# Narrower one-hot blocks and larger bursts in a fused Fourier-mixing and expert kernel

## The chip, the cores and the metric

The kernel runs on one core of a Trainium2 chip. The metric is the device time of one execution in microseconds (us). Engines are named as in the profile: PE (TensorE, matrix multiply; PEld are its weight loads), DVE (VectorE), ACT (ScalarE), POOL (GpSimd) and SP (SyncE, which mostly issues DMAs). Lines L1 to L1303 are those of the kernel before, unless the text says that they are of the changed one.

## What is computed

The output is a gated sum of two branches on the same input x of 2048 tokens and 640 features.

```python
g = sigmoid((x * gate_w).sum(-1, keepdims=True))
a = dft_seq_re @ (x @ dft_hid_re.T) - dft_seq_im @ (x @ dft_hid_im.T)
# branch b, for each token and each of 32 heads:
s1 = q1 @ k1.T ; s2 = q2 @ k2.T        # 16 scores each
t1, i1 = top2(s1) ; t2, i2 = top2(s2)  # 4 pairs, expert i1 * 16 + i2 of 256
top_s, top_e = top2(t1[:, None] + t2)  # the best 2 of the 4 pairs
w = softmax(top_s)
b = sum over heads and 2 picks of w * gelu(x . u[top_e]) * v[top_e]
out = g * a + (1 - g) * b
```

The change lies in branch b, in one step. For every token, the 64 weights w (32 heads, 2 picks) have to be added up into a table of 16 x 16 experts, at row i1 and column i2 of each pick. Everything behind it (gelu, the product with v) then works on that dense table.

## The kernel before, in words

**Large matmuls.** Nearly all of PE's time goes into float32 products written as three matmuls on split operands (`mm3`, L143 to L145): a high times a high part, a high times a low, a low times a high. The order of the program is the order of the *pieces*: 128 pieces of the sequence transform, each with five groups of three matmuls of 512 columns (`seq_piece`), which accumulate in the PSUM banks 0 to 4. Sixteen pieces make one tile; at its end ACT copies the five banks into `ST` (L246), DVE multiplies them by the gate (L217), and ACT issues their stores (L227). Behind the pieces comes the hidden-dimension transform (`step`), which ends the kernel.

**Operands of a piece.** `load_piece` loads `wf` five pieces ahead (SP, L177). `split_piece` makes the high and the low part in `WS` three pieces ahead: either ACT and POOL (L138, L139), or ACT twice (L188, L189) and then a DMA issued by POOL which adds `wf` from DRAM (L191).

**Background work.** What is not a large matmul is written as generators and queued in a `Pump`. `run_bg(0.68)` after each group of three matmuls adds credit, and the pump takes the next step of a generator as long as there is credit; each step yields its price in us (the *charge*). So the charges decide between which matmuls a step's instructions are written into the program, and each engine then runs its own instructions in that order. `at(n, ...)` ties a step to piece n.

**The one-hot step** (`experts`, L802 to L886). `ROWS[g]` holds, for half g of the tokens, three numbers for each of 128 partitions (pick, head, and a split of the weight in two) and token: a power of two that stands for the row expert, one for the column expert, and the weight. A *set* is 64 tokens. `build` makes two f16 matrices of 1024 columns for a set with three DVE instructions (L845): each token's 16 columns say which power of two its number equals, and the row expert's matrix is also multiplied by the weight. `use` multiplies block by block on PE (L857): a block is four tokens, 16 x 4 = 64 columns, so a set is 16 matmuls of 64 columns with 64 output partitions, alternating between partitions 0 to 63 and 64 to 127. A block's product holds all 4 x 4 pairs of its tokens; only a token with itself is wanted. So ACT multiplies the bank by a mask, one column of tokens at a time (L815, four instructions of 128 elements for a set), and DVE adds over the four token columns (L821, one reduction for a set) into `cd`. `store_gates` (L796, SP) writes `cd` to DRAM.

Sets are used in bursts: three built sets give one burst of 48 matmuls on PE, in banks 6, 7 and 5, each set in a bank of its own. There are four set buffers in two tiles, `hot0` and `hot1`; the latter lies under the tag `WP`, which is needed from piece NPC - 4 on, so that groups have two sets near the end (`ending`). `settle`, called after every build instruction, writes the sum of one masked set and the mask of the next. `closing` holds masks back in the last piece of a tile, `early` tells of pieces below `ACCUM_END`, where builds are charged less.

Of the kernel before, what the change touches and what calls it, by code (L numbers as in the profile page):

```python
# [17 lines left out]
P = 128  # L18
# [23 lines left out]
AWAY = 11  # L42
BYPASS = 4
# [63 lines left out]
def gated_mix_kernel(ctx: ExitStack, tc: tile.TileContext, xT, xn, dreT, dimT, wsre, wsim, wq, kT, uT, vv, gw, out):  # L107
# [97 lines left out]
    p3, last_part, ending, closing, early, share = None, False, False, False, True, 0.95  # L205
# [133 lines left out]
    wtab4 = const.tile([P, E, 4], F16)  # L339
    powers = const.tile([P, E], F16)  # L340
    top_bits = const.tile([P, 1], F32)
    mask4 = const.tile([P, 4], F32)
# [9 lines left out]
    def make_tables():  # L352
        for e in range(E):
            nc.gpsimd.memset(powers[:, e:e + 1], 2.0 ** (E - 1 - e))
        nc.gpsimd.memset(top_bits, INF)
        nc.gpsimd.tensor_copy(wtab4, powers[:, :, None].to_broadcast([P, E, 4]))
        nc.vector.tensor_reduce(mask4, identf.rearrange("p (a b) -> p b a", b=4), op=OP.add, axis=AX.X)
        nc.vector.tensor_scalar(mask4, mask4, 1.0 / GSCALE, None, op0=OP.mult)
# [443 lines left out]
    def experts():  # L802


        shp = [P, 16, E, 4]
        wt = wtab4[:, None].to_broadcast(shp)
# [5 lines left out]
        def mask(t):  # L812
            f = t.rearrange("p m (e t) -> p (m e) t", t=4)
            for n in range(4):
                nc.scalar.activation(f[:, :, n], f[:, :, n], AF.Copy, scale=mask4[:, n:n + 1])  # L815

        def add_up(g, c, t):
# [3 lines left out]
            nc.vector.tensor_reduce(cd[g][:, :, 8 * c:8 * c + 8].rearrange("p e m -> p m e"),  # L821
                                    t.rearrange("p m (e t) -> p m e t", e=E), op=OP.add, axis=AX.X)
            if c == 15:
# [11 lines left out]

        def build(g, c, s):
            pt, qt = (HOT[s // 2][:, s % 2, n].rearrange("p (m e t) -> p m e t", e=E, t=4) for n in range(2))

            def row(n):
                r = ROWS[g][:, n, 8 * c:8 * c + 8, :].rearrange("p b (s t) -> p (b s) t", t=4)  # L840
# [3 lines left out]
            for o, a, b, op in ((pt, row(0), wt, OP.is_equal), (qt, row(1), wt, OP.is_equal), (pt, pt, row(2), OP.mult)):  # L844
                nc.vector.tensor_tensor(o, a, b, op=op)  # L845
                yield (0.8 if early else 1.05) + settle()

        def use(group):
# [3 lines left out]
            for i, (g, c, s) in enumerate(group):  # L852
                t = bank((6, 7, 5)[i], (P, 8, E * 4))
                pt, qt = (HOT[s // 2][:, s % 2, n].rearrange("p (m c) -> p m c", m=16) for n in range(2))
                for m in range(16):
                    r = slice(64 * (m % 2), 64 * (m % 2) + 64)
                    nc.tensor.matmul(t[r, m // 2, :], pt[:, m], qt[:, m], start=True, stop=True)  # L857
# [446 lines left out]
```

## Time and profile before

| | |
|---|---|
| median of 3 executions | 750.1 us (749.87 to 751.22) |
| the profiled execution | 750.43 us |
| span of its instructions | 748.7 us |
| granted PE clock | 0.999 |
| PE / PEld busy | 743.8 / 603.8 us |
| DVE / ACT / POOL busy | 585.7 / 365.9 / 342.4 us |
| matmuls of the one-hot step (L857) | 512, from 419.6 to 587.6 us |
| builds, masks, sums (L845, L815, L821) | 96, 128, 32 instructions |

The span runs from the first to the last instruction on the engines; 1.7 us lie around it. Busy time counts instructions on an engine, also those that overlap in its pipeline, so that a busy PE is not PE at its peak. In a row of a group stand the line, the engine and operation, what is written and read, the count, then busy us and mean ns of one, then the engine's idle time ahead of them and what ended it. In a row of the chain or of the timeline stand start and length in us.

### The profile page before, as it was taken

To read this page: it belongs to the slowest core of one execution; us is meant where nothing else is said; L and a number is where in the kernel's file an instruction comes from. 1 tells how busy PE (TensorE), PEld (TensorE's weight loads), DVE (VectorE), ACT (ScalarE), POOL (GpSimd) and SP (SyncE) were. 2 spreads that over 40 slices of the span, in tenths; PEclk is the share of its full clock that TensorE was granted. 3 is DMA by queue.
4 is the path that set the end of the run, shared out by engine and by line. 5 is a ranking of instruction groups with operands and counts; after the bars stand their busy time and mean duration, and the time that the engine had idled before them with its cause. 6 is when DMAs were issued, how large, how long until landed. Compare 5 with 4: busy or idle time off the path is not lost.

```text
span 748.7 us, 11141 instructions
## 1 busy us (share of the span) xinstructions
PE 743.8 (99%) x3925; PEld 603.8 (81%) x3925; DVE 585.7 (78%) x741; ACT 365.9 (49%) x664; POOL 342.4 (46%) x286
## 2 busy tenths in 40 slices
PE   9999999999999999999999999999999999999998
PEld 7777767888888888888888888888888888888887
DVE  6964098495999899999999888979899974357651
ACT  4325234543544745555463686633545653443451
POOL 5533325440532424145235456643455793487253
PEclk9999999999999999999999999999999999999999
DMA  9999999777556786972398766488876689775301
GB/s 333 392 380 364 344 374 354 231 222 250 129 176 141 190 242 157 237 200 79 114 395 285 162 168 188 133 255 280 266 234 197 222 262 343 219 239 172 113 29 71
DMA packets 84488, 171.11 MB, mean 229 GB/s; under 512 B 16080, under 2 KB 21328, under 8 KB 84176
## 3 DMA queue, kind: packets, MB, share of 16 engines
q1 hardware_dynamic: 70960, 146.13, 57.9%
q0 software_dynamic: 5472, 9.96, 8.5%
q10 hardware_dynamic: 8000, 14.31, 5.2%
q8 instruction: 31, 0.51, 0.3%
q14 instruction: 25, 0.20, 0.1%
HBM read 136.40 MB, written 32.39 MB: 225 GB/s over the span
## 4 chain that ended last, share of the span: by engine, by line
PE 94%; DMA 5%; SPq 0%; DVE 0%; ACT 0%; issue 0%; ACTq 0%
PE b L143 30%; PE b L145 30%; PE b L144 30%; PE b L239 2%; DMA wf<-in_wsre 2%; PE b L380 2%; DMA wq<-in_wq 1%; PE b L857 1%; DMA xd<-X 1%; DMA gdr<-gc 1%; DVE wp L386 0%; SPq L177 0%; ACT WS L295 0%; ACTq L514 0%; DVE ST L1191 0%
## 5 line engine op out<-in xcount | busy, mean ns | idle before, releaser
L143 PE MATMUL b<-WS,X 128*128 128x512 f32 x620 | 243.3, 392 | 0.0
L144 PE MATMUL b<-WS,X 128*128 128x512 f32 x620 | 241.4, 389 | 0.0
L145 PE MATMUL b<-WS,X 128*128 128x512 f32 x620 | 241.3, 389 | 0.0
L139 POOL TENSOR_TENSOR WS<-wf,WS 128x512 fp32r<-128x512 f32 x89 | 131.9, 1486 | 168.3 <-ACT WS L138 151.8
L143 PEld LDWEIGHTS b<-WS,X 128*128 128x128 f32 x620 | 116.3, 188 | 28.2 <-issue 4.1
L145 PEld LDWEIGHTS b<-WS,X 128*128 128x128 f32 x620 | 116.4, 188 | 24.4
L144 PEld LDWEIGHTS b<-WS,X 128*128 128x128 f32 x620 | 116.4, 188 | 23.6
L138 ACT ACTIVATE WS<-wf 128x512 fp32r<-128x512 f32 x89 | 55.5, 626 | 69.0 <-PE b L145 40.9
L845 DVE TENSOR_TENSOR hot<-rows,wtab 128x1024 f16<-128x1024 f16 x64 | 57.8, 930 | 4.3 <-PE b L857 4.3
L139 POOL TENSOR_TENSOR xl<-xf,xh 128x640 fp32r<-128x640 f32 x16 | 27.2, 1702 | 72.0 <-ACT xh L138 72.0
L567 ACT ACTIVATE sc<-b 128x512 f32<-128x512 f32 x32 | 19.9, 621 | 80.8 <-PE b L145 77.0
L191 POOL DMA_DIRECT2D WS<-in_wsre x30 | 26.4, 881 | 61.8 <-ACT WS L189 60.5
L139 POOL TENSOR_TENSOR WS<-ra,WS 128x512 fp32r<-128x512 f32 x33 | 47.1, 1439 | 14.3 <-ACT WS L138 14.1
L815 ACT ACTIVATE b<-b,mask 128x128 f32<-128x128 f32 x128 | 43.1, 342 | 14.9 <-PE b L857 11.8
L138 ACT ACTIVATE WS<-ra 128x512 fp32r<-128x512 f32 x47 | 29.4, 631 | 42.4 <-PE b L145 29.6
L622 DVE TENSOR_TENSOR eq<-sc,mm 128x1024 f16<-128x1024 f32 x32 | 44.4, 1387 | 0.9
L629 DVE TENSOR_REDUCE tied<-eq 128x64 f32<-128x1024 f16 x32 | 39.0, 1219 | 0.9
L620 DVE TENSOR_REDUCE mm<-sc 128x64 f32<-128x1024 f32 x32 | 38.7, 1211 | 0.2
L139 POOL TENSOR_TENSOR WP<-ra,WP 128x512 fp32r<-128x512 f32 x13 | 19.2, 1490 | 31.0 <-ACT WP L138 30.9
L217 DVE SCALAR_TENSOR_TENSOR ST<-ST,grow 128x512 f32<-128x512 f32 x40 | 31.7, 855 | 1.7 <-ACT tw L138 1.7
L845 DVE TENSOR_TENSOR hot<-hot,rows 128x1024 f16<-128x1024 f16 x32 | 31.6, 986 | 0.0
L143 PE MATMUL b<-WU,xh 128*128 128x512 f32 x80 | 31.1, 389 | 0.0
(209 smaller groups left out, 1449.1 us busy)
## 6 DMA issues: line engine op xcount, KB each, us to landing
X<-xd SPq DMA_DIRECT2D x36, 640.0 KB, 6.5
wq<-in_wq SPq DMA_DIRECT2D x32, 640.0 KB, 7.1
wf<-in_wsim SPq DMA_DIRECT2D x64, 256.0 KB, 4.8
wf<-in_wsre SPq DMA_DIRECT2D x63, 256.0 KB, 6.4
ra<-pd SPq DMA_DIRECT2D x40, 256.0 KB, 3.3
pd<-ST ACTq DMA_DIRECT2D x35, 256.0 KB, 5.6
WS<-in_wsre POOLq DMA_DIRECT2D x30, 256.0 KB, 6.0
xd<-X SPq DMA_DIRECT2D x11, 640.0 KB, 9.1
```

The lines of the kernel that those rows point to most:

```text
L138: nc.scalar.activation(h, f, AF.Copy)
L139: eng.tensor_sub(l, f, h.bitcast(F32))
L143: nc.tensor.matmul(o, wh, ah, start=first, stop=False, skip_group_check=more)
L144: nc.tensor.matmul(o, wh, al, start=False, stop=False, skip_group_check=more)
L145: nc.tensor.matmul(o, wl, ah, start=False, stop=last, skip_group_check=more)
L191: nc.gpsimd.dma_start(l, (wsre, wsim)[w][c, s], accum_op=OP.add)
L217: nc.vector.scalar_tensor_tensor(f, f, -1.0 if w else 1.0, g, op0=OP.mult, op1=OP.mult)
L620: nc.vector.tensor_reduce(m, sc, op=OP.max, axis=AX.X)
L622: nc.vector.tensor_tensor(eq, sc, m[:, :, None].to_broadcast([P, HH, E]), op=OP.is_equal)
L629: nc.vector.tensor_reduce(tied[:, s, ib, :], eq, op=OP.add, axis=AX.X)
L815: nc.scalar.activation(f[:, :, n], f[:, :, n], AF.Copy, scale=mask4[:, n:n + 1])
L845: nc.vector.tensor_tensor(o, a, b, op=op)
```

## The change

Blocks shrink from four tokens to two (`TB = 2`): 32 columns with 32 output partitions, four blocks side by side on the 128 partitions (`CG = 4`), 32 matmuls for a set. Two sets share one PSUM bank, in its two halves; one mask (two instructions of 256 elements) and one sum (16 x 16 outputs of 2 elements) serve both. Banks 5, 6 and 7 are taken in rotation. A group is four sets, always an even number, and two near the end. A fifth buffer is added: while the first half of the tokens is built it is the tile under the tag `xl`, once all rows are there and before `late`; for the second half it is the memory of `ROWS[0]`, which is used up by then. `settle` is called once for a set, after its last build instruction. A build instruction is charged 0.9 in place of 0.8 while `early`. `store_gates` issues four DMAs for a half in place of two, as the tables lie on four times 32 partitions.

```diff
+TB = 2
+MS = 64 // TB
+CG = P // (TB * E)
@@ store_gates
-            for s in range(2):
-                nc.sync.dma_start(gd[g][s].rearrange("t e f m -> e t f m"), summed[g][64 * s:64 * s + 64])
+            for s in range(CG):
+                n, t = divmod(TB * s, 4)
+                nc.sync.dma_start(gd[g][n, t:t + TB].rearrange("t e f m -> e t f m"),
+                                  summed[g][TB * E * s:TB * E * (s + 1)])
@@ mask, add_up
-            f = t.rearrange("p m (e t) -> p (m e) t", t=4)
-            for n in range(4):
-                nc.scalar.activation(f[:, :, n], f[:, :, n], AF.Copy, scale=mask4[:, n:n + 1])
+            f = t.rearrange("p m (e t) -> p (m e) t", t=TB)
+            for n in range(TB):
+                nc.scalar.activation(f[:, :, n], f[:, :, n], AF.Copy, scale=mask_t[:, n:n + 1])
-            nc.vector.tensor_reduce(cd[g][:, :, 8 * c:8 * c + 8].rearrange("p e m -> p m e"),
+            nc.vector.tensor_reduce(cd[g][:, :, 8 * c:8 * c + 16].rearrange("p e m -> p m e"),
@@ new: which buffers are free
+        def free_now():
+
+            if todo[0][0] == 1:
+                if not HOT[4:] or HOT[4][0] == 0:
+                    if HOT[4:] and 4 not in free_sets:
+                        return [s for s in free_sets if s < 2 or not ending]
+                    if not HOT[4:]:
+                        HOT.append(None)
+                        free_sets.append(4)
+                    HOT[4] = 1, ROWS[0].rearrange("p a b c -> p (a b c)")[:, :16 * P].rearrange("p (n c) -> p n c", n=2)
+            elif not HOT[4:] and not late and len(rowed) == NT:
+                HOT.append((0, big.tile([P, 2, 16 * P // 2], F16, name="hot4", tag="xl")))
+                free_sets.append(4)
+            return [s for s in free_sets if s not in ((2, 3) if ending else (4,) if late and todo[0][0] == 0 else ())]
@@ build
-                yield (0.8 if early else 1.05) + settle()
+                yield (0.9 if early else 1.05) + (settle() if op == OP.mult else 0.0)
@@ use
-                t = bank((6, 7, 5)[i], (P, 8, E * 4))
-                for m in range(16):
-                    r = slice(64 * (m % 2), 64 * (m % 2) + 64)
-                    nc.tensor.matmul(t[r, m // 2, :], pt[:, m], qt[:, m], start=True, stop=True)
-                unmasked.append((g, c, t))
+                if i % 2 == 0:
+                    t = bank(5 + rotate("hot", 3), (P, 16, E * TB))
+                    unmasked.append((g, c, t))
+                for m in range(MS):
+                    r = slice(TB * E * (m % CG), TB * E * (m % CG + 1))
+                    nc.tensor.matmul(t[r, 8 * (i % 2) + m // CG, :], pt[:, m], qt[:, m], start=True, stop=True)
@@ groups
-            while todo and len(group) < (2 if ending else 3):
+            while todo and (len(group) < (2 if ending else 4) or len(group) % 2):
@@ main loop
-        ending, closing, early = n >= NPC - 7, n % NT == NT - 1, n < ACCUM_END
+        ending, closing, early, late = n >= NPC - 7, n % NT == NT - 1, n < ACCUM_END, n >= NT * (NC + 2) - 10
```

Three places show how the order of instructions moves. The first is PE's entry into the first burst: rows of a large matmul's three parts, then weight load and matmul of the first block. Before:

```order
L143 MATMUL b_3092<-WS,X 128x512
L144 MATMUL b_3092<-WS,X 128x512
L145 MATMUL b_3092<-WS,X 128x512
L857 LDWEIGHTS hot_3457
L857 MATMUL b_3556<-hot_3457 64x64
```

Now (`mm3` is L146 to L148 there, the one-hot matmul L883):

```order
L146 MATMUL b_3089<-WS,X 128x512
L147 MATMUL b_3089<-WS,X 128x512
L148 MATMUL b_3089<-WS,X 128x512
L883 LDWEIGHTS hot
L883 MATMUL b_3576<-hot 32x32
```

The output of a block shrinks from 64 x 64 to 32 x 32, and the burst goes from 48 such pairs of rows to 128. It stands two groups of three matmuls later than before (after bank b_3089's in place of b_3092's of the piece ahead); the whole program has 8 bursts of 128 in place of ten of 48 and one of 32.

The second place is DVE from the first build on: builds (L845) write `hot` from `rows`, sums (L821) write `cd` from a bank, L217 is the gate's product. Before:

```order
L845 TENSOR_TENSOR hot_3458<-rows_1232,wtab_158 128x1024 x2
L845 TENSOR_TENSOR hot_3458<-hot_3458,rows_1232 128x1024
L845 TENSOR_TENSOR hot_3457<-rows_1232,wtab_158 128x1024 x2
L821 TENSOR_REDUCE cd<-b_3556 128x8x16
L845 TENSOR_TENSOR hot_3457<-hot_3457,rows_1232 128x1024
L845 TENSOR_TENSOR hot_3457<-rows_1232,wtab_158 128x1024 x2
L845 TENSOR_TENSOR hot_3457<-hot_3457,rows_1232 128x1024
L821 TENSOR_REDUCE cd<-b_3573 128x8x16
L845 TENSOR_TENSOR hot_3458<-rows_1232,wtab_158 128x1024
L821 TENSOR_REDUCE cd<-b_3590 128x8x16
L217 SCALAR_TENSOR_TENSOR ST<-ST,grow 128x512 x5
```

Now (L869, L826 and L220 in the changed kernel):

```order
L869 TENSOR_TENSOR hot<-rows_1232,wtab 128x1024 x2
L869 TENSOR_TENSOR hot<-hot,rows_1232 128x1024
L869 TENSOR_TENSOR hot<-rows_1232,wtab 128x1024
L220 SCALAR_TENSOR_TENSOR ST<-ST,grow 128x512 x5
L869 TENSOR_TENSOR hot<-rows_1232,wtab 128x1024
L869 TENSOR_TENSOR hot<-hot,rows_1232 128x1024
L826 TENSOR_REDUCE cd<-b_3576 128x16x16
L869 TENSOR_TENSOR hot<-rows_1232,wtab 128x1024 x2
L869 TENSOR_TENSOR hot<-hot,rows_1232 128x1024
L826 TENSOR_REDUCE cd<-b_3641 128x16x16
```

The first sum moves from inside the fifth set to behind the seventh and behind the gate's product, and a sum stands once in two sets.

The third place is ACT behind the second and third masks of the first tile. ST's stores (`pd<-ST`), the halves of a piece (`WS<-wf`, `WS<-WS`) and the masks (`b<-b,mask`) stand with the semaphores that they wait for: DMAHW0 to DMAHW7 tell of earlier DMAs' landings, and each new DMA takes over one of these eight lanes from an older one. Before:

```order
L227 DMA pd_73<-ST 128x512 [waits DMAHW5_49,DVE_49]
L138 ACTIVATE WS<-wf 128x512 [waits DMAHW3_49,PE_49,Pool_49]
L721 ACTIVATE rows_1233<-lb 128x384 [waits DMAHW7_49,DMAHW1_49,DMAHW0_49]
L227 DMA pd_73<-ST 128x512 [waits DMAHW6_49,DVE_49]
L138 ACTIVATE DD<-draw 128x640
L188 ACTIVATE WS<-wf 128x512 [waits DMAHW2_49,PE_49]
```

Now (L230 is the store, L191 and L192 the halves, L820 the mask):

```order
L724 ACTIVATE rows_1233<-lb 128x384 [waits DMAHW7_49,DMAHW0_49]
L820 ACTIVATE b_3856<-b_3856,mask_t 128x256 [waits PE_49]
L820 ACTIVATE b_3856<-b_3856,mask_t 128x256 [waits Activation_49]
L230 DMA pd_73<-ST 128x512 [waits DMAHW4_49,DVE_49]
L141 ACTIVATE DD<-draw 128x640
L191 ACTIVATE WS<-wf 128x512 [waits DMAHW3_49,PE_49]
```

The store before waited for lane DMAHW6, now for DMAHW4, which a load of `wf` (L177) holds at that point; a mask of the third pair now stands just ahead of it.

More of the change, by code (lines that the diff above doesn't have):

```diff
@@ L802, in experts @@
     def experts():
-        shp = [P, 16, E, 4]
-        wt = wtab4[:, None].to_broadcast(shp)
+        shp = [P, MS, E, TB]
+        wt = wtab[:, None].to_broadcast(shp)
         todo = deque((g, c) for g in range(2) for c in range(16))
@@ L865, in experts @@
             group = []
-            while todo and len(group) < (2 if ending else 3):
-                free = [s for s in free_sets if s < 2 or not ending]
-                if prev and (not free or ending and any(s > 1 for g, c, s in prev)):
+            while todo and (len(group) < (2 if ending else 4) or len(group) % 2):
+                free = free_now()
+                if prev and (not free or ending and any(s in (2, 3) for g, c, s in prev)):
                     yield from use(prev)
```

31 lines of the change are left out of this document (18 added, 13 removed).

## The prediction

> **What bounds the kernel now.** I read the page's busy shares first, then the chain that ended last, then the chain in order of time, and last one burst in the timeline.
>
> ```profile
> PE 743.8 (99%) x3925; PEld 603.8 (81%) x3925; DVE 585.7 (78%) x741; ACT 365.9 (49%) x664; POOL 342.4 (46%) x286
> ...
> PE 94%; DMA 5%; SPq 0%; DVE 0%; ACT 0%; issue 0%; ACTq 0%
> PE b L143 30%; PE b L145 30%; PE b L144 30%; PE b L239 2%; DMA wf<-in_wsre 2%; PE b L380 2%; DMA wq<-in_wq 1%; PE b L857 1%; DMA xd<-X 1%; DMA gdr<-gc 1%; DVE wp L386 0%; SPq L177 0%; ACT WS L295 0%; ACTq L514 0%; DVE ST L1191 0%
> ```
>
> TensorE carries 94% of the chain, and the changed line, L857, stands in it with about 1%. So whatever VectorE or ScalarE save is worth nothing by itself. The change can win only in the one-hot bursts on TensorE, and it can lose wherever it makes TensorE wait. How long a burst is, the chain in order of time tells (start, length, what):
>
> ```profile
> 28.66 2.29 PE b L380 x32
> ...
> 419.71 0.88 PE b L857 x48
> 420.59 0.43 PE b L143
> ...
> 571.11 0.88 PE b L857 x48
> ...
> 587.17 0.62 PE b L857 x32
> ```
>
> There are eleven bursts: ten of 48 matmuls (three sets) and a last one of 32. Sixteen matmuls more cost 0.88 - 0.62 = 0.26 us, 16.3 ns each, or 32.5 ns for the two that stand on the two halves of the columns. 48 x 16.3 ns is 0.78, so 0.10 of the 0.88 belongs to the burst and not to its matmuls. The timeline of TensorE around the first burst shows two more such costs:
>
> ```profile
> 418.87 0.39 PE L143 MATMUL b<-WS,X 128*128 128x512 f32 x1
> 419.09 0.39 PE L144 MATMUL b<-WS,X 128*128 128x512 f32 x1
> 419.32 0.39 PE L145 MATMUL b<-WS,X 128*128 128x512 f32 x1
> 419.64 0.95 PE L857 MATMUL b<-hot 128*64 128x64 f16 x48
> 420.52 0.50 PE L143 MATMUL b<-WS,X 128*128 128x512 f32 x1
> 420.85 0.39 PE L144 MATMUL b<-WS,X 128*128 128x512 f32 x1
> ```
>
> Ordinary starts are 0.23 us apart. Into the burst it is 0.32, and from the first matmul behind it to the second 0.33, so entry and exit add 0.09 and 0.10. A burst therefore costs 0.10 + 0.09 + 0.10 = 0.29 us fixed plus 16.3 ns per matmul: 1.07 us with 48, 0.81 with 32. **All eleven cost 10 x 1.07 + 0.81 = 11.5 us.** That is the whole sum from which the change can take.
>
> **The change, part by part.** *Bursts.* The changed order has 8 bursts of 128 matmuls, each of 32 columns on 32 output partitions. Three fixed costs go: 3 x 0.29 = 0.9 us. What a group of four such matmuls costs (one on each quarter of the columns, 32 groups in a burst) no row shows. The nearest is the pair above. If a group streams its columns and nothing else, it takes half of a pair, 16.3 ns. If a step costs the same whatever its columns, 32.5 ns. If every matmul keeps its 16.3 ns, four take 65 ns. L380 speaks for the low part: its 32 matmuls, also on quarters of 32 partitions but with 320 columns, take 2.29 us, 286 ns for four, while one matmul of 512 columns takes 230. 320 columns in that ratio would be 144 ns, 570 for four in a row, so the four quarters do run beside each other. That leaves 16.3 to 32.5, and I take the middle, 24.4 ns. A burst is then 0.29 + 32 x 24.4 ns = 1.07 us, what a burst of three sets costs now, and the eight cost 8.6. **Gain 11.5 - 8.6 = 2.9 us.** At the ends: 8 x 0.81 = 6.5 us (gain 5.0) and 8 x 1.33 = 10.6 (gain 0.9); at 65 ns, 8 x 2.37 = 19.0 (7.5 lost).
>
> The Trainium skill has a rule against this step: "TensorEngine Tiling (Array Packing)", section "Instruction Overhead", gives every matmul about 60 cycles, so that one column takes as long as 60, and advises against tiling a dimension that is already small. No run here has 32 columns; the 16.3 ns per matmul above shows that it cannot hold for each matmul apart, only for each group, which is my upper end of 32.5 ns and the second rival below.
>
> *VectorE and ScalarE.* The stretch in which the bursts lie (length, then busy us of PE, its weight loads, DVE, ACT, POOL):
>
> ```profile
> 408.00:600.00 192.00, 192.00 (x1308) 157.24 (x1307) 173.99 (x221) 110.78 (x248) 102.36 (x74) 1.00 0.69 211
> ```
>
> The operations that change, and one of 512 elements to compare with (busy us, mean ns):
>
> ```profile
> L845 DVE TENSOR_TENSOR hot<-rows,wtab 128x1024 f16<-128x1024 f16 x64 | 57.8, 930 | 4.3 <-PE b L857 4.3
> L845 DVE TENSOR_TENSOR hot<-hot,rows 128x1024 f16<-128x1024 f16 x32 | 31.6, 986 | 0.0
> L815 ACT ACTIVATE b<-b,mask 128x128 f32<-128x128 f32 x128 | 43.1, 342 | 14.9 <-PE b L857 11.8
> L821 DVE TENSOR_REDUCE cd<-b 128x128 f32<-128x512 f32 x32 | 21.7, 684 | 11.2 <-ACT b L815 10.9
> L567 ACT ACTIVATE sc<-b 128x512 f32<-128x512 f32 x32 | 19.9, 621 | 80.8 <-PE b L145 77.0
> ```
>
> Sums halve from 32 to 16, each still reading 512 elements: 16 x 0.68 = 10.9 us less on VectorE (twice the outputs could make one dearer, at most like the 1024-element reduction below, 1.21 us, which gives 8.5 of it back). Masks go from 128 of 128 elements to 32 of 256: between 0.34 and 0.62 us, by the line through both 0.44, so 43.1 us become about 14. None of it is on the chain: VectorE is busy 174.0 of these 192 us and would have some 29 free. It is only cover.
>
> The 96 builds keep their 1024 elements, but the repeated operand is now two f16 (one 32-bit word) read sixteen times, where it was four. The nearest row is L622, which reads one f32 word sixteen times, beside L620, a plain pass over as many elements (minimum, median, maximum ns):
>
> ```profile
> L620 DVE TENSOR_REDUCE mm<-sc x32: 1199/1210/1221, 150.4 to 394.2; 128x64 f32<-128x1024 f32 x32
> L622 DVE TENSOR_TENSOR eq<-sc,mm x32: 1210/1225/2544, 151.7 to 395.5; 128x1024 f16<-128x1024 f32 x32
> ```
>
> 1225 against 1210: reading one word again and again costs nothing visible, so I take the builds as unchanged. The upper end is L620's pace of one element at a time, 1.21 us where the median build is about 0.68: 96 x 0.53 = 51 us more.
>
> The skill speaks against this too: "Vector Engine (DVE) Microarchitecture Reference", section 5.2 "Measured stream behaviour on trn2 (trn3 not measured)", has a port at full rate only in runs of two adjacent 4-byte words, 1.73 against 1.05 ns per column where one source hops at every element. An estimate by those figures is 512 x 0.68 ns = 0.35 us more per build, 33 us in all; L622's 1225 ns against 1210 disagrees with it, as long as the word is the same one.
>
> *Order.* In the changed order all twelve builds of four sets, and most of a fifth set's three, stand before the gate multiplications (L217) on VectorE; VectorE then has to wait for TensorE to free a set. The build that comes last before a burst is followed by one set's builds of slack, as now. Charges, wtab and mask table cost nothing that shows: the tables are made once in phase one. Storing the gates takes four issues per half in place of two, on SP, about 0.38 us each; nothing in the burst region waits for that queue's issue time.
>
> *A new wait.* With the masks thinned out, ScalarE reaches its stores of ST (L227) at other places, and their semaphore lanes are dealt anew. The store behind the third pair of masks must now wait for lane DMAHW4, held by a wf load that SP issues shortly before; of the stores there now, the nearest wait for older transfers. Behind it on ScalarE stand a DD split and the two halves of a WS piece, and behind those POOL's accumulating load. From the timeline of ScalarE:
>
> ```profile
> 444.11 0.62 ACT L188 ACTIVATE WS<-wf 128x512 fp32r<-128x512 f32 x1
> 444.77 0.63 ACT L189 ACTIVATE WS<-WS 128x512 fp32r<-128x512 f32 x1
> ```
>
> The instructions on WS between 430 and 470 us (minimum, median, maximum ns), and how long its accumulating loads took to land:
>
> ```profile
> L191 POOL DMA_DIRECT2D WS<-in_wsim x4: 875/882/906, 430.7 to 453.6; - x4
> DMA to landing us min/median/max: 4.2/4.9/6.6
> ```
>
> And the loads of wf on SP's queue between 430 and 460 us:
>
> ```profile
> L177 SPq DMA_DIRECT2D wf<-in_wsim x9: 328/382/1204, 438.5 to 458.5; - x9
> DMA to landing us min/median/max: 3.6/4.8/6.9
> ```
>
> From L188 to the landing it takes 1.3 + 0.9 + 4.9 = 7.1 us, and a piece is begun three pieces ahead, 3 x 15 x 0.23 = 10.3 us. Slack 3.2 us. A wf load takes 4.8 us to land (up to 6.9); ScalarE spends about 0.9 on the two masks ahead of the store. So TensorE may wait 4.8 - 0.9 - 3.2 = 0.7 us. Ends: nothing, if the load has landed by then, and 6.9 - 3.2 = 3.7. I take **0.7 us lost**.
>
> **Sum.** -2.9 + 0.7 = -2.2 us. The profiled execution took 750.4 us (span 748.7 and 1.7 around it) and comes to 748.2; the median shown, 750.1, is 0.3 lower and comes to **747.9 us**.
>
> **The rivals.** *Narrow blocks, no gain from narrowness* (a group of four costs what a pair costs): 10.6 us of bursts, gain 0.9, less the wait of 0.7: 749.9. For it: the pair's 32.5 ns is more than its columns need by the 230 ns of 512 (64 columns in that ratio are 29), so a part of the step need not shrink. *Better than forecast*: 16.3 ns a group and no wait, 745.1.
>
> *The issue of matmuls becomes the bound* (slower): 256 instructions, loads and matmuls, in one burst. The 16.3 ns per load and matmul of today bound the rate only from one side; if they are its limit, 8 bursts cost 19.0 us and the kernel 750.1 + 7.5 = 757.6. It decides from 8.9 ns per matmul on (8 x (0.29 + 128 x 8.9 ns) = 11.5). Against it: the pair's 32.5 ns is close to what its 64 columns need by the 512-column rate (29 ns), which leaves little for an issue limit today.
>
> *ScalarE held longer* (slower): if two stores meet such a lane at the upper end, 2 x 3.7 - 2.9 = +4.5, 754.6; it decides from 2.9 us of waits. *Builds slow down* (slower): VectorE has 29 us of cover, so it decides from 0.30 us per build; at the upper end 51 - 29 = 22 us, about 770. That the change doesn't do what it says is excluded by the order, which has the 8 bursts, 32 masks and 16 sums.
>
> **How the numbers follow.** Forecast 0.46 (747 to 749.2), better 0.12, no gain from narrowness 0.18, issue 0.11, ScalarE held 0.07, builds 0.06. About 0.2% (1.5 us) is what a measurement of this kernel can tell from no change. Faster: 0.39 of the forecast, 0.12, and 0.01 of the narrow case, 0.52. Same: 0.07 of the forecast and 0.15 of the narrow case, 0.22. Slower: the last three and 0.02 of the narrow case, 0.26. The range is 745.5 to 752.5: it takes in the better case nearly to its end, the narrow one and the mild ends of the slower ones, and leaves out most of the last three. The forecast's own range is 747 to 749.2.
>
> **What would show it.** Lines are those of the changed kernel. Bursts: L883 as 128 matmuls with 0.88 us from the first to L146 (about 6 ns a matmul; 1.14 for the narrow rival, over 2 for the issue rival). Builds: median 0.68 us at L869. Masks 0.44, sums 0.68. The wait: a gap of 0.4 to 1 us on TensorE at an L147, between 450 and 462 us, that ends with a landing in WS; ScalarE idle some microseconds ahead of a store. I am wrong if the bursts together exceed 10 us, or if TensorE waits more than 2 us in that stretch or at any other.

## The result, and the profile after

The changed kernel takes 754.4 us in the median of seven executions (752.4 to 756.4), the kernel before 750.1. The ratio is 1.0054, with a 95% interval of 1.0041 to 1.0067: **slower by about 4 us**. The forecast was 747.9 us with a range of 745.5 to 752.5, so the sign was wrong as well as the size. The profiled execution of the changed kernel is its mildest one, 752.39 us with a span of 750.6.

The page after, in the rows that answer to those of before:

```profile
PE 743.8 (99%) x4437; PEld 604.4 (81%) x4437; DVE 581.7 (78%) x725; ACT 337.0 (45%) x568; POOL 345.0 (46%) x286
...
PE 91%; DMA 6%; SPq 1%; ACT 1%; issue 0%; POOL 0%; DVE 0%; ACTq 0%
...
L147 PE MATMUL b<-WS,X 128*128 128x512 f32 x620 | 241.4, 389 | 1.6 <-DMA WS<-in_wsim 1.6
```

ScalarE got 29 us lighter and VectorE 4, and it bought nothing. What is new is the last row: a large matmul waits for a piece of WS, and DMA's share of the chain rises from 5% to 6%. The bursts in the chain in order of time (start, length), the first, an ordinary one and the last:

```profile
421.37 1.22 PE b L883 x128
...
473.13 1.19 PE b L883 x128
...
574.06 1.15 PE b L883 x128
```

A burst of 128 takes 1.19 us where the forecast had 0.88. With entry and exit as before (0.09 and 0.11) it costs 1.39 us, and the eight together 11.1. The eleven bursts of before cost 10 x 1.07 + 0.81 = 11.5 by the same reading, so narrowness and length together gained 0.4 us and not 2.9.

Masks and sums came out close to their forecast:

```profile
L820 ACT ACTIVATE b<-b,mask_t 128x256 f32<-128x256 f32 x32 | 15.0, 472 | 0.9 <-PE b L883 0.3
L826 DVE TENSOR_REDUCE cd<-b 128x256 f32<-128x512 f32 x16 | 10.9, 682 | 6.1 <-ACT b L820 6.1
```

The builds' rows show why VectorE gained 4 us and not the 10.9 of the sums (minimum, median, maximum ns, as in the rows of L845 they replace):

```profile
L869 DVE TENSOR_TENSOR hot<-rows,wtab x56: 674/683/2249, 410.4 to 544.9; 128x1024 f16<-128x1024 f16 x56
L869 DVE TENSOR_TENSOR rows<-rows,rows x4: 1773/1784/2028, 473.0 to 559.1; 128x1024 f16<-128x1024 f16 x4
```

The median build is unchanged, but more of them fall on slow moments: 30 of the 96 take over 0.9 us, 26 before, and all four products in the fifth buffer are among them. In both traces each of these slow builds ends 0.54 to 0.56 us after the end of a TENSOR_TENSOR of POOL that overlaps it, and no build that overlaps none of POOL's is slow.

And TensorE around the new wait, from its timeline:

```profile
453.32 0.39 PE L146 MATMUL b<-WS,X 128*128 128x512 f32 x1
455.34 0.50 PE L147 MATMUL b<-WS,X 128*128 128x512 f32 x1 [1.63 <-DMA WS<-in_wsim]
455.68 0.40 PE L148 MATMUL b<-WS,X 128*128 128x512 f32 x1
```

Two starts that should be 0.23 us apart are 2.02 apart: 1.79 us lost. Followed back from there, the chain in order of time reads:

```profile
440.49 6.35 DMA wf<-in_wsim
...
446.92 0.33 ACTq L230
...
447.29 0.75 ACT DD L141
...
448.11 1.51 POOL DD L142
449.62 5.68 DMA WS<-in_wsim
...
455.34 0.50 PE b L147
```

Read it from the bottom. The piece landed at 455.30 because POOL issued its accumulating load at 449.62, behind a split of DD. That split waited for ScalarE, and ScalarE had stood still in front of a store of ST (L230) until a load of wf landed at 446.84. ScalarE's own timeline shows the pause:

```profile
440.83 1.26 ACT L820 ACTIVATE b<-b,mask_t 128x256 f32<-128x256 f32 x2
446.92 0.33 ACTq L230 DMA_DIRECT2D pd<-ST  x1
447.29 0.74 ACT L141 ACTIVATE DD<-draw 128x640 fp32r<-128x640 f32 x1 [5.20 <-DMA wf<-in_wsim]
447.93 0.61 ACT L191 ACTIVATE WS<-wf 128x512 fp32r<-128x512 f32 x1
448.58 0.63 ACT L192 ACTIVATE WS<-WS 128x512 fp32r<-128x512 f32 x1
```

The masks end at 442.1, the store goes out at 446.92: 4.8 us in which ScalarE does nothing. The store needs nothing from that load. They share a lane, that is, a semaphore that counts landings. The program deals eight lanes to the transfers of the hardware queues in turn, and a transfer must not go out before the last one on its lane has landed. Here is the piece of that deal (place in the order, queue, line, what, lane):

```
299 SP  L180 wf    DMAHW3      304 SP  L719 lb (transpose)  DMAHW0
300 SP  L180 wf    DMAHW4      305-307 SP L180 wf           DMAHW1-3
301 ACT L230 pd    DMAHW5      308 ACT L230 pd              DMAHW4 <- waits for 300
302-303 SP L719 lb DMAHW6-7    309-310 SP L921 draw         DMAHW5-6
```

Store 308 stands exactly eight places behind load 300; in the trace both carry the same semaphore number. SyncE issued that load late, at 440.49, since three transposes, two draw loads and load 299 stood ahead of it on its queue. It then took 6.35 us to land.

### The profile page after: what moved, and what is told of

The parts are those of the page before. It is cut to its first block, busy times and chain, and to the rows that moved or that the text cites. A ratio compares the mean times of both kernels' runs of the same rounds, so it can differ in the third digit from the quotient of the medians.

```text
span 750.6 us, 12044 instructions
## 1 busy us (share of the span) xinstructions
PE 743.8 (99%) x4437; PEld 604.4 (81%) x4437; DVE 581.7 (78%) x725; ACT 337.0 (45%) x568; POOL 345.0 (46%) x286
## 4 chain that ended last, share of the span: by engine, by line
PE 91%; DMA 6%; SPq 1%; ACT 1%; issue 0%; POOL 0%; DVE 0%; ACTq 0%
PE b L146 29%; PE b L147 29%; PE b L148 29%; PE b L242 2%; PE b L383 2%; DMA wq<-in_wq 1%; DMA wf<-in_wsre 1%; DMA xd<-X 1%; PE b L883 1%; DMA wf<-in_wsim 1%; DMA WS<-in_wsim 1%; DMA gdr<-gc 1%; PE b L329 1%; SPq L719 0%; SPq L180 0%; ACT rows L724 0%
## 5 line engine op out<-in xcount | busy, mean ns | idle before, releaser
L146 PE MATMUL b<-WS,X 128*128 128x512 f32 x620 | 243.1, 392 | 0.0
L147 PE MATMUL b<-WS,X 128*128 128x512 f32 x620 | 241.4, 389 | 1.6 <-DMA WS<-in_wsim 1.6
L148 PE MATMUL b<-WS,X 128*128 128x512 f32 x620 | 241.3, 389 | 0.0
L146 PEld LDWEIGHTS b<-WS,X 128*128 128x128 f32 x620 | 116.4, 188 | 28.1 <-issue 3.1
L147 PEld LDWEIGHTS b<-WS,X 128*128 128x128 f32 x620 | 116.4, 188 | 25.7 <-DMA WS<-in_wsim 2.1
L148 PEld LDWEIGHTS b<-WS,X 128*128 128x128 f32 x620 | 116.4, 188 | 24.4
L869 DVE TENSOR_TENSOR hot<-rows,wtab 128x1024 f16<-128x1024 f16 x56 | 53.3, 986 | 10.3 <-PE b L883 10.3
L220 DVE SCALAR_TENSOR_TENSOR ST<-ST,grow 128x512 f32<-128x512 f32 x40 | 31.8, 850 | 2.3 <-DMA grow<-gdr 1.8
L146 PE MATMUL b<-WU,xh 128*128 128x512 f32 x80 | 31.1, 389 | 0.0
L147 PE MATMUL b<-WU,xh 128*128 128x512 f32 x80 | 31.1, 389 | 0.0
L148 PE MATMUL b<-WU,xl 128*128 128x512 f32 x80 | 31.1, 389 | 0.0
```

Source lines behind the costliest of these rows:

```text
L146: nc.tensor.matmul(o, wh, ah, start=first, stop=False, skip_group_check=more)
L147: nc.tensor.matmul(o, wh, al, start=False, stop=False, skip_group_check=more)
L148: nc.tensor.matmul(o, wl, ah, start=False, stop=last, skip_group_check=more)
L220: nc.vector.scalar_tensor_tensor(f, f, -1.0 if w else 1.0, g, op0=OP.mult, op1=OP.mult)
```

## The experiments

Three theories of the loss were put against each other first. **A**: the lane holds ScalarE, so the piece is late, so TensorE waits. **B**: the bursts of four sets and the new order of builds make that stretch late by themselves. **C** puts it on the bursts' own cost.

**e1: another lane for the same store.** One transfer of 256 bytes is put ahead of the store, so that the deal moves on by one place.

```diff
+    spare = dram.tile([1, 64], F32, name="spare", tag="spare")
 ...
         for d in chunks:
+            if (q, d) == (NC, 3):
+                nc.sync.dma_start(spare, xn[0, :1, :64])
             eng.dma_start(pd[w, c][d], staged.pop((q, d)))
```

> The changed kernel with one extra transfer of 256 bytes (from xn to a DRAM tile that nobody reads), issued by SyncE just ahead of the fourth store of the second half's ST (the one that ScalarE could not issue from 440.8 to 446.9 us). Counters are dealt to transfers in turn, eight of them, so that store now inherits its counter from another store that ended long before, and no longer from the wf load issued at 440.5 us. Nothing else changes. Theory A (the store's inherited wait holds ScalarE, the split of the next piece is late, and TensorE waits for it): ScalarE's pause after 440 us is gone, no wait for WS above 0.5 us between 448 and 460 us, and the time falls by 1.8 us (the profiled wait) to 4.5 us: 749.5 to 751.5, about what the kernel before takes. Rival B (the four-set bursts and the new order of builds make the pieces of that stretch late by themselves): 753 to 755.5 and TensorE still waits for WS there. Rival C (the bursts of 32-column matmuls cost more than the trace of one run shows): 753 to 755.5 without a wait for WS there.

Measured: 751.04 us (750.42 to 752.08), a ratio of 1.001 to the kernel before (1.0001 to 1.0019). ScalarE's timeline at the same place:

```profile
440.92 1.26 ACT L823 ACTIVATE b<-b,mask_t 128x256 f32<-128x256 f32 x2
442.66 0.34 ACTq L233 DMA_DIRECT2D pd<-ST  x1
443.05 0.74 ACT L141 ACTIVATE DD<-draw 128x640 fp32r<-128x640 f32 x1 [0.87 <-DVE hot L872]
446.30 0.63 ACT L191 ACTIVATE WS<-wf 128x512 fp32r<-128x512 f32 x1 [2.51 <-DMA wf<-in_wsim]
```

The store goes out at 442.66 instead of 446.92 and the DD split no longer stands behind it. No matmul waits for WS any more. With one transfer that nobody reads the kernel is 3.2 us faster than e4 below, so A holds, and B and C fall for this loss; 0.7 us to the kernel before stay.

The last row shows something else: ScalarE still idles, by 2.51 us, now for the load of the piece that it is to split (place 299 in the deal). In the changed kernel, too, that load lands only at 445.92. So only a part of the 4.8 us counted: POOL issues the piece's accumulating load at 448.00 here and at 449.62 there, 1.62 us apart, where TensorE lost 1.79. And there was no slack to take it up, for even here a weight load waits 0.2 us for WS.

**e4: the changed kernel once more**, unchanged, beside e1.

> The changed kernel once more, beside the three others: 752.4 to 756.4, median about 754.4. Theory A: where this execution is longer than the first one's 752.4, the wait for WS between 448 and 460 us is longer than 1.8 us by the difference. Rivals: the difference sits in the bursts, or is spread over the span.

Measured: 754.25 us (752.81 to 754.8), and the profiled execution is the median one, 1.86 us longer than the first profile. TensorE's timeline:

```profile
453.65 0.39 PE L146 MATMUL b<-WS,X 128*128 128x512 f32 x1
457.26 0.50 PE L147 MATMUL b<-WS,X 128*128 128x512 f32 x1 [3.23 <-DMA WS<-in_wsim]
```

And the end of the chain in order of time:

```profile
448.63 1.52 POOL DD L142
450.15 7.07 DMA WS<-in_wsim
457.26 0.50 PE b L147
```

The gap is 3.61 - 0.23 = 3.38 us, 1.59 more than in the first profile. The chain gives the same sum: POOL issues 0.53 later (450.15 for 449.62), its load takes 1.39 longer (7.07 for 5.68), and TensorE comes to the place 0.33 later (453.65 for 453.32). The difference of these two executions is thus mostly that of this wait; about 0.3 us of the 1.86 lie elsewhere.

The wait is not all that spreads the times. Both profiles have the full TensorE clock, but eight of the twelve executions of the changed kernel show a mean granted clock of 0.995 to 0.998 and took 753.2 to 756.4 us; the four with 1.000 took 752.4 to 754.3. The kernel before has 0.999 or 1.000 in all 54 executions beside the experiments. What lies behind this the next trace shows.

**e7: settling after every instruction again.** The narrow blocks and the four-set bursts stay. ScalarE's masks stand at other places, but the store still falls on the lane of that load.

```diff
-                yield (0.9 if early else 1.05) + (settle() if op == OP.mult else 0.0)
+                yield (0.9 if early else 1.05) + settle()
```

> The changed kernel with settling put back to after every instruction of a build; narrow blocks, four-set bursts and charges stay, and in this order, too, the fourth store of ST inherits its counter from the wf load that SyncE issues behind its transposes. Theory A: ScalarE is held again for 3 us or more with that load as the releaser, TensorE waits 1 to 4 us for WS between 448 and 460 us, and the time is 752.5 to 755.5. Rival F (settling once per set is what makes the piece late, by masks that come in a lump): no wait for WS there, 750.5 to 751.5.

Measured: 753.63 us (753.31 to 755.13). TensorE waits for WS, and its chain is:

```profile
439.15 5.96 DMA wf<-in_wsim
...
445.19 0.36 ACTq L230
...
447.93 2.06 issue
449.99 5.44 DMA WS<-in_wsim
```

The same load, a hold again (masks end at 442.1, the store goes out at 445.19) and again a late piece. How the masks are settled is not what makes it late. The row "issue" adds 2.06 us that are not the hold itself: POOL's split of DD took 3.64 us there in place of 1.57, while VectorE made five builds without a break (445.5 to 448.6). In e1, without a hold, the split began at 443.87; that the hold moved it among these builds is likely, but not shown.

Behind the wait this execution shows what the two profiles above do not. TensorE's timeline, and three stretches of 2 us (length, then busy us of PE, its weight loads, DVE, ACT and POOL, then the granted clock):

```profile
455.47 0.71 PE L147 MATMUL b<-WS,X 128*128 128x512 f32 x1 [2.30 <-DMA WS<-in_wsim]
...
454.00:456.00 2.00, 0.53 (x2) 0.41 (x2) 0.00 (x0) 0.00 (x0) 2.00 (x2) 0.90 1.01 311
456.00:458.00 2.00, 2.00 (x131) 1.43 (x130) 0.96 (x2) 0.64 (x2) 0.17 (x1) 0.50 1.08 281
458.00:460.00 2.00, 2.00 (x7) 1.64 (x8) 2.00 (x4) 1.07 (x3) 0.00 (x0) 0.75 0.65 202
```

The clock is halved for some 3.4 us. From this L147 to the second L146 behind it, over the burst, TensorE takes 3.65 us; in the changed kernel's profile it takes 2.66. So the wait can cost 1.0 us more than its own length. A mean of 0.998 is what 3.4 us at half clock make of 752 us, so the untraced executions with such a mean probably had a stretch like it.

**e3: the old charge of 0.8.** A smaller charge moves the store in the deal, to eight places behind a draw load.

```diff
-                yield (0.9 if early else 1.05) + (settle() if op == OP.mult else 0.0)
+                yield (0.8 if early else 1.05) + (settle() if op == OP.mult else 0.0)
```

> The changed kernel with the old charge of 0.8 for an early build in place of 0.9. In this order the store of ST that was held inherits its counter from a draw load, issued some 2 us ahead of the wf loads, and no longer from a wf load. Theory A: ScalarE is held less (0 to 3 us in place of 6), and the time is 749.5 to 752. Rival B and C: the four-set bursts of narrow matmuls are all there, so 753 to 755.5.

Measured: 751.84 us (750.36 to 752.67), and no wait of TensorE for WS. Bursts, blocks and settling are all there: one number of a charge, which costs no time in itself, takes most of the loss away. The lanes are dealt anew, and the store goes out 0.9 us after the masks; the charge also moves builds and bursts, so this run alone does not part the two. What stays lies in the bursts, which have pauses and take 12.7 us together; TensorE's waits show 1.0 of it (us in total, times, the longest):

```profile
PE b L883 <- DVE hot L869: 1.0, 2, 0.5
```

**e9: the store from SyncE's queue**, the fix without an extra transfer.

```diff
-        eng = nc.sync if q == 2 * NC - 1 else nc.scalar
+        eng = nc.sync if q == 2 * NC - 1 or (q, *chunks) == (NC, 3) else nc.scalar
```

> The changed kernel, whole, with one line more: the fourth store of the second half's ST goes out from SyncE's queue and no longer from ScalarE's. It then stands ahead of the next three wf loads, and inherits its counter from an older store; no transfer is added. Theory A: ScalarE is not held after 440 us (it goes on with the draw split, at the latest when its data is there), TensorE waits for WS there by less than 0.5 us, and the time is that of e1 and e5, 750.4 to 751.6; the gain of the bursts (0.45 us by the profiles) is below what the comparison can tell. Rival H (the store itself, 0.6 us of SyncE's time ahead of the wf loads, makes these late instead): a wait for WS or wf between 452 and 470 us and 752 to 754.

Measured: 751.07 us (749.76 to 754.26), ratio 1.0014 (1.0002 to 1.0026), no wait for WS. It is e1's time by another way, and rival H falls. Four of its twelve executions took 752.4 us or more; the profiled one is not among them, so what they waited for is open.

**e8: a shorter chain behind the held store.** The hold stays; the DD split behind it goes to the next piece.

```diff
-            at(N1 + 6 + 5 * m + 2 * a, split_dd, m, a)
+            n = N1 + 6 + 5 * m + 2 * a
+            at(n + 1 if n == NT * (NC + 1) + 4 else n, split_dd, m, a)
```

> The changed kernel (store held as it is) with one split of the draw tile, the one that stands on ScalarE between the held store and the split of the late piece, moved one piece later. Its ScalarE half takes 0.64 us there, and its GpSimd half (1.5 us) stands ahead of the transfer that completes the piece. Theory A: the chain from the held store to the landing in WS loses both, 0.64 us on ScalarE and about 0.4 us on GpSimd, so TensorE's wait for WS falls by about 1.05 us: from 1.6 to 3.2 us to 0.5 to 2.2 us, and the time to 751.4 to 753.4 with a median near 753.2. Rival G (the piece is late because its own wf load or the DMA engines are late, not by the chain behind the store): 753.8 to 754.8, the wait as before.

Measured: 753.59 us (752.52 to 754.75), less of a gain than A expected. The piece did come in time: POOL issues at 449.37, and no matmul waits for WS. But another wait took its place, in the burst right behind:

```profile
454.20 0.97 PE L883 MATMUL b<-hot 128*32 128x32 f16 x96
456.58 0.38 PE L883 MATMUL b<-hot 128*32 128x32 f16 x32 [1.41 <-DVE hot L869]
```

Where the fourth set was, VectorE's timeline shows:

```profile
446.06 0.68 DVE L869 TENSOR_TENSOR hot<-hot,rows 128x1024 f16<-128x1024 f16 x1
451.57 0.69 DVE L826 TENSOR_REDUCE cd<-b 128x256 f32<-128x512 f32 x1 [4.84 <-ACT b L820]
452.18 2.66 DVE L869 TENSOR_TENSOR hot<-rows,wtab 128x1024 f16<-128x1024 f16 x2
454.76 1.76 DVE L869 TENSOR_TENSOR hot<-hot,rows 128x1024 f16<-128x1024 f16 x1
```

ScalarE's pause also delays its next masks. Their sum stands on VectorE ahead of the last set's builds, so VectorE idles 4.84 us. In the changed kernel it idles 5.01 us at the same place, unseen: its set is ready at 455.41, and TensorE, which waits for WS until 455.34, comes to the burst at 456.00. In e8 TensorE comes 1.8 us earlier. There two of the set's three builds are slow (2.06 and 1.76 us for the usual 0.68; in the changed kernel one is), so the set is ready at 456.5. The burst after it waits 1.47 us for its last set, this time with VectorE busy throughout, on builds of up to 3.8 us; together that is 2.9 us. At the first burst two waits ran side by side, and taking away the one uncovered the other. Theory A was right on the chain behind the store and wrong on what a shorter chain is worth. Only freeing ScalarE removes both.

**e2: the kernel before, settled once per set.** Blocks of 64 columns and three-set bursts; here, too, a store falls on the lane of a load of wf.

```diff
-                yield (0.8 if early else 1.05) + settle()
+                yield (0.8 if early else 1.05) + (settle() if op == OP.mult else 0.0)
```

> The kernel before, with one part of the change alone: masks and sums are settled once per set and no longer after every instruction of a build. Blocks stay 64 columns wide, bursts stay at 3 sets, charges stay at 0.8. In this order, too, the store of ST inherits its counter from a wf load issued behind a crowded SyncE queue. Theory A: ScalarE is held after 440 us for 3 us or more with that load as the releaser, TensorE then waits for WS by 448 to 460 us, and the time is 752 to 755, though not one matmul differs. Rivals B and C (the cost sits in the four-set bursts or in the narrow matmuls, of which there is none here): 749.6 to 750.6.

Measured: 759.32 us (759.08 to 760.28), ratio 1.0124. That is slower than A expected, and not for A's reason: ScalarE idled 1.7 us for the load, and TensorE did not wait for WS. The row among TensorE's waits (us in total, times, the longest):

```profile
PE b L857 <- DVE cd L821: 6.5, 9, 2.2
```

One of them on VectorE's timeline:

```profile
460.72 0.69 DVE L821 TENSOR_REDUCE cd<-b 128x128 f32<-128x512 f32 x1 [3.39 <-ACT b L815]
```

And the same moment on TensorE's:

```profile
460.49 0.70 PE L857 MATMUL b<-hot 128*64 128x64 f16 x32
461.47 0.44 PE L857 MATMUL b<-hot 128*64 128x64 f16 x16 [0.28 <-DVE cd L821]
```

Three sets fill three banks. With one settling per set the last set of a burst is summed only right before the next burst, and that burst's third set needs the same bank: TensorE waits for the sum, nine times. Two sets to a bank make a burst need two of the three banks, and the changed kernel has no such wait. So settling once per set and two sets to a bank belong together. As a test between A and B this run told nothing.

**e5: twice the columns, the same instructions.** The lane is shifted as in e1. Nearly every one-hot matmul streams 64 columns in place of 32 (its own block and the next one's, which the next group overwrites).

```diff
-                    nc.tensor.matmul(t[r, 8 * (i % 2) + m // CG, :], pt[:, m], qt[:, m], start=True, stop=True)
+                    j, w = 8 * (i % 2) + m // CG, 2 if m < MS - CG else 1
+                    nc.tensor.matmul(t[r, j:j + w, :], pt[:, m], qt[:, m:m + w], start=True, stop=True)
```

> The changed kernel with the extra transfer of e1 (so without ScalarE's pause; 751.0 to compare with), and every one-hot matmul but the last four of a set streams 64 moving columns in place of 32: its own block and the next one's, whose place in the bank the next group of four overwrites with the right block. The count of weight loads and matmuls and what ends in the bank are the same; the columns streamed are nearly doubled. Theory A (once TensorE's queue has run empty, after some 36 matmuls, a burst goes at the pace at which instructions arrive, 8.35 ns for a weight load with its matmul, whatever they do): groups of four stay near 33 to 35 ns, a burst stays within 0.1 us of e1's (first to last start 1.09 to 1.2 us), and the time is 751 to 752. Rival D (the array's work on a block sets the pace, as the sum of the prediction had it): groups go to 60 ns or more, a burst to 2 us, and the time is 757 to 759.

Measured: 750.8 us (749.6 to 755.29), ratio 1.0008 (0.9995 to 1.002). The columns are all but free. One burst in the timeline, to be held against 1.19 us between the starts of L883 and L146:

```profile
439.57 1.28 PE L887 MATMUL b<-hot 128*32 128x64 f16 x128
440.77 0.50 PE L146 MATMUL b<-WS,X 128*128 128x512 f32 x1
```

1.20 us. Why is seen in the starts of the single matmuls in the trace. The distance from each group of four to the next, in ns, over the second burst (for before: from each pair to the next):

```
before  (pairs)  53 31 32 32 31 32 32 31 32 32 31 32 32 31 32 32 31 32 32 31 32 32 31
after            39 25 25 25 25 25 25 29 33 36 33 34 33 33 34 56 37 33 34 32 34 34 33 56 37 33 33 33 34 33 33
e5               40 29 29 29 29 29 30 29 28 28 34 33 33 34 33 56 37 33 33 34 33 33 34 55 36 34 33 33 34 33 33
```

There are two paces. At first groups come 25 ns apart with 32 columns, 29 with 64. Then both kernels go at 33 to 34 ns a group whatever is streamed: 8.35 ns for a weight load with its matmul, 4.2 ns per instruction. (The two 56s hold the last matmul of the second and of the third set, which starts 24 ns late.) Rival D falls: the columns do not set the second pace.

What does? The change of pace comes after 33 matmuls in the one and after 41 in the other, so it is no fixed count. But the later groups lie on one line in both. Followed back at 33.4 ns a group, that line passes the burst's first matmul 49 ns before it starts in the one (218 ns for the first eight groups, less 8 x 33.4) and 33 ns before in the other (301 less 10 x 33.4). This is how a steady supply looks, with a head start of one to one and a half groups, which a faster array uses up sooner. The single starts look like it too: in the fast part the four matmuls of a group start 3 to 4 ns apart and a pause follows, in the slow part each starts 8.3 ns after the one ahead of it. So the second pace is most likely the rate at which instructions reach the array; that is an inference, only the columns are excluded by a run. The Trainium skill, "TensorE: Matmul & The Clock Gate", section "Architectural detail: the array is 16× 32×32, not 1× 128×128", gives TensorE a queue of 64 instructions. Were it full of one-hot work when a burst begins, the fast pace would last for all 32 groups by the same working; the head start seen is some 8 to 12 instructions (up to 17 if the first set, too, spent 24 ns at its last matmul).

**e6: bursts of two sets**, with the lane shifted as in e1.

```diff
-            while todo and (len(group) < (2 if ending else 4) or len(group) % 2):
+            while todo and (len(group) < 2 or len(group) % 2):
```

> The changed kernel with the extra transfer of e1 and bursts of two sets: 16 bursts of 64 matmuls in place of 8 of 128, the same matmuls. Theory A (the first 36 matmuls of a burst, queued while the products ahead still run, start 6.25 ns apart, the rest 8.35 ns): first to last start is 36 x 6.25 + 27 x 8.35 = 0.45 us, a burst costs TensorE 0.19 us more than that, 0.64 us, 16 of them 10.3 us, the same as 8 of 1.28: 750.8 to 752. Rival E (one pace of 8.56 ns throughout and a fixed part of 0.19 us a burst): 0.54 us from first to last, 0.73 each, 11.7 in all: 752.2 to 753.5.

Measured: 752.88 us (752.57 to 753.53), so A's time was wrong and E's right. That is 1.84 more than e1, 1.7 by the ratios (the kernel before took 0.4 more beside this run). A burst of 64:

```profile
440.46 0.68 PE L886 MATMUL b<-hot 128*32 128x32 f16 x64
441.07 0.50 PE L146 MATMUL b<-WS,X 128*128 128x512 f32 x1
```

First to last start is 0.50 us, between A's 0.45 and E's 0.54. With entry and exit a burst costs 0.80 us: 0.30 fixed and 0.50. Sixteen cost 12.8, against 11.1 for eight of 128: 1.7 us. Both expectations had left out 0.11 us per burst, the late second matmul behind it. With that added A's sixteen cost 0.9 us more than eight long ones and E's 2.3; the measured 1.7 lies between them, and neither model is right in its numbers. The two paces of e5 do give the length of a burst: 218 ns for its first eight groups, 31 x 8.35 behind them and 24 ns at the set's last matmul are 0.50 us.

## Why the prediction was wrong, step by step

- **"All eleven cost 11.5 us", and 0.29 us fixed per burst.** Right. e6 gives 0.30 fixed at another length.
- **"I take the middle, 24.4 ns" per group of four, gain 2.9.** This step failed first. The average over a burst is 8.6 ns per matmul, 34 ns per group, just above the upper end of 32.5 that I allowed. The burst's start agrees with it (25 ns), but that holds for eight groups of 32. The rule of the Trainium skill weighed there ("TensorEngine Tiling (Array Packing)", "Instruction Overhead") does not hold for each matmul, as the prediction said; what its cycles count per group the traces don't show, and behind the first eight groups something else binds. Measured gain: 0.4 us.
- **The rival "the issue of matmuls becomes the bound".** Its mechanism is the likeliest reading of the second pace, at 8.35 ns per load and matmul. The prediction had it decide from 8.9 ns on, so it turned the gain into nearly nothing, not into a loss. My argument against it (64 columns need about what the pair costs) only said that today's bursts are not limited by it. It said nothing of a burst with half the work per instruction.
- **VectorE, ScalarE and builds.** Off the path, as said. Masks 0.47 us on average, sums 0.68. The builds' median stayed, 683 ns against 681, so the rule of the Trainium skill weighed there ("Vector Engine (DVE) Microarchitecture Reference", section 5.2) does not bite where the same word is read again. Their mean grew (53.3 + 28.3 + 6.4 + 7.4 us for 96, against 57.8 + 31.6), which took back 6 us of what the sums gave.
- **The new wait, "0.7 us lost", 0 to 3.7.** Place, lane, load and releaser were right, and it is what makes the kernel slower: e1 and e9 remove it and most of the loss. Its size was wrong. The prediction's sum is the hold, plus the chain from ScalarE's first half of the piece to the landing, less the lead of that half: 3.9 + 7.1 - 10.3 = 0.7 us. The first profile has 4.8 + 7.4 - 10.4 = 1.8, e4 has 4.6 + 8.8 - 10.0 = 3.4. Two landings were mis-sized: the load of wf took 6.35 us (7.08 in e4) and not 4.8, the accumulating load 5.68 (7.07) and not 4.9. POOL's split of DD, which stood in my list, was not in the sum and adds 0.4 us behind ScalarE's halves; against that, POOL's 0.9 us of issuing was counted twice, as the landing times run from the start of the issue. The upper end of 3.7 left out the 0.9 us of masks that the middle took off. Nor was the slack of 3.2 us there to be used: e1, without the hold, has the piece only just in time. That a wait can be followed by half the clock (e7) was not in the sum at all. The decision point given for the rival "ScalarE held longer", 2.9 us, assumed the gain of 2.9; with a gain of 0.4 any wait above that decides.
- **The sum.** -0.4 for the bursts and +1.8 for the wait make +1.4 us; the two spans differ by 1.9. Of the rest, TensorE is 0.3 us later already ahead of the first burst, and from its last matmul to the end it is 3.86 us in place of 3.60. In e4: -0.4 + 3.4 = 3.0 of 3.8.

Without the hold the changed kernel should be 0.4 us faster than before by its bursts, yet e1, e5 and e9 stand at ratios of 1.001, 1.0008 and 1.0014. A lane takes part of it here, too: that of the last store. Its issue on SyncE's timeline, first before (span 748.7 us), then in the changed kernel (750.6):

```profile
745.86 0.34 SPq L1192 DMA_DIRECT2D out_y<-ST  x1
...
747.57 0.34 SPq L1217 DMA_DIRECT2D out_y<-ST  x1
```

From there to the end it is 2.80 us before (and in e2), but 3.04 to 3.10 in all nine traces of the changed kernel and its variants. The program ends with SyncE checking its lanes one after the other, 0.06 us each. The store stood on the last lane but one of this row; now it stands on the fourth or fifth of nine, and the checks behind it come after its landing. In e1's trace, moreover, two bursts take 0.24 and 0.13 us longer than the others, with pauses between their sets. What is left is some tenths of a microsecond, less than single executions differ by. No version run here beats the kernel before.

## What to carry to other kernels

A transfer can be held by one it has nothing to do with, if both count on the same semaphore; so when an edit moves stores and loads past each other, write down which lane each gets and who had it before, and look for a late load in front of an engine that the critical path needs. Price such a hold to the end of its chain, with every instruction that stands behind the held one on each queue, and at the upper end of the landing times, since the lane is taken by whichever transfer is slow. And before cutting matmuls into smaller ones, count instructions as well as columns: a pace seen with larger tiles bounds the supply of instructions only from one side.

## What the runs showed of the hardware that was not expected

- Matmuls of 32 columns on quarters of the array come at 25 ns for four of them over the first 33 of a burst, and 8.35 ns apart behind that. With 64 columns it is 29 ns for four over the first 41, and the same 8.35 behind (e5).
- The same transfer of 256 KB into WS took 5.68 us in one execution and 7.07 in another of the same program (e4), so a hold by a lane differs from run to run by more than the bursts gained.
- Builds of 0.68 us took up to 2.2 us each, in both kernels, and all of the slow ones (26 and 30) end 0.54 to 0.56 us behind a TENSOR_TENSOR of POOL. In e7 it was POOL's split that took 3.64 us in place of 1.57 beside five builds. The two engines seem to take turns; no run moved the one away from the other.
- After TensorE had idled 2.30 us in e7, its granted clock was 0.50 for some 3.4 us; after 1.63 and 3.23 us in the two profiles of the changed kernel it stayed at 1.00.
